# Moving 46 of 96 up-projection units of an MLP into the attention loop before it, with the intermediate kept in DRAM scratch

## The chip, the cores and the metric

One core of a Trainium2 chip runs the whole program. The metric is device time in microseconds (us), the median of several executions. The kernel before takes about 370 us. In runs on a single core an execution counts as slow when it is over 1.5% above the fastest of its kernel.

Engine names in the profile: PE is the matmul engine (PEld its weight loads), DVE the vector engine, ACT the engine for exp and tanh, SP the engine that issues most DMAs.

## The reference, cut to what matters

```python
# attention: B=4, H=8 heads, S=768, D=64; block-sparse mask (blocks of 32)
scores = where(mask, q @ k.T / sqrt(D), -1e9)
attn   = softmax(scores);  out = attn @ v
x = out.transpose(0, 2, 1, 3).reshape(3072, 512)
# MLP
h = x @ w_in                        # 3072 x 2048
g = h * (1 / (1 + exp(-beta * h)))
return g @ w_out                    # 3072 x 512
```

The kernels write the third line as h * (1 + tanh(beta * h / 2)) and take the factor 0.5 into `w_out`; so their MLP needs a tanh and a multiply.

## The kernel before

It first runs a loop over the 32 (batch, head) pairs, here called heads, and then the MLP, here called the tail. All operands of matmuls are fp16. The parts that matter:

```python
# PSUM of the attention loop: 4 banks scores, 2 tp, 1 av, 1 xtp = all 8
scores_pool (bufs=2), tp_pool (bufs=2), av_pool (bufs=1), xtp_pool (bufs=1)

for idx in range(n_bh + 1):
    # ... load q, k, v; cast; 6 + 6 PE transposes of q and k into tp tiles, copy to qa, ka ...
    for kc in range(6):
        sc = scores_pool.tile([128, 768], FP32)
        # two matmuls, 512 and 256 columns
        nc.scalar.activation(out=et[:, kc, :], in_=sc, func=AF.Exp, scale=SCALE)
    # of the previous head: 36 AV matmuls, reciprocal, scale into xstage;
    # every second head: 6 PE transposes of xstage
    xtp = xtp_pool.tile([128, 6, 128], FP16, tag="xtp")
    # ... transposes into xtp, copied to xT_sb (x transposed, all in SBUF)

attn_psum_ctx.close()
for tg in range(6):                     # 512 tokens each
    for ffc in range(16):               # one "unit": 4 matmuls of 512 columns
        # hp (PSUM) = w_in chunk x xT
        nc.scalar.activation(out=t_sb, in_=hp, func=AF.Tanh, scale=beta_h_sb[:, ffc])
        nc.vector.scalar_tensor_tensor(out=g_sb[:, ffc, :], in0=t_sb, scalar=1.0,
                                       in1=hp, op0=ALU.add, op1=ALU.mult)
    for tsub in range(4):               # 16 matmuls g x w_out, copy, store
        ...
```

The kernel's framework puts the instructions of each engine into an order of its own, by a static plan, and it is not that of the program text. A tile's buffers are handed out in rotation within its pool and tag.

The softmax here doesn't subtract the row's maximum and nothing guards it: scores larger than these inputs give would overflow.

## Time and profile before

| stretch of the profiled run (368.8 us) | length | what sets its pace |
|---|---|---|
| loading, mask, first transposes | 25 us | DMA, dependencies |
| attention loop, to the last scaled output at 198.3 us | 173 us | ACT: 5.12 us per head (heads 10 to 31) |
| tail | 170 us | PE: 12 blocks of 64 matmuls, 13.8 us each |

"Us per head" here and below is the mean distance between the instructions that scale the attention output, from the 10th to the 31st of them. "Attention ends" is the start of the 32nd.

The page of the kernel before, its second part: the busy share of each engine in 40 slices of the span, in tenths.

```profile
PE   0338999898999999999998999999999999999995
ACT  0035889777899888889985812812812812812810
DMA  7995364788444453645300002002002002002002
```

Up to slice 21 ACT is the engine that is nearly full; after it PE is, and ACT works only in bursts. The PE row shows nine tenths in attention too, but matmuls overlap in it: a matmul of 512 columns is recorded as 382 ns long, while the next one starts after 216 ns. The Trainium skill, "Perfetto Trace Analysis", section "Identifying the Most-Contended Engine", warns that matmul busy time says little about how near PE is to its limit; the table of stretches agrees here, because PE is "busy" 71 of 74 us while ACT sets the pace:

```profile
110.00:184.00 74.00, 71.24 (x921) 48.55 (x918) 37.26 (x104) 66.03 (x89) 0.00 (x0) 1.00 0.49 111
198.50:365.20 166.70, 166.62 (x773) 75.35 (x771) 82.87 (x122) 65.95 (x96) 0.00 (x0) 1.00 0.10 37
```

The columns are: stretch, length, then busy us and number of instructions of PE, PEld, DVE, ACT and POOL, the granted PE clock, the DMA share and GB/s. In the second row PE has no hole: the tail is PE work from end to end. The chain of waits, in order of time, says the same at its end:

```profile
323.68 13.81 PE op L195 x64
337.49 13.81 PE hp L181 x64
351.30 13.83 PE op L195 x64
```

64 matmuls in 13.81 us are 216 ns each, so a unit is 0.86 us.

### The profile page before, as it was taken

What the parts mean: (1) busy time and instruction counts of PE and PEld (TensorE: products, weight loads), DVE (VectorE), ACT (ScalarE), POOL (GpSimd) and SP (SyncE); (2) the same over time, 40 slices, a digit from 0 to 9 for tenths busy, and PEclk for the clock granted to TensorE, in tenths of its full rate; (3) what the DMA queues carried; (4) which work ended last, traced back from release to release, by engine and by line L of the source; (5) the groups of instructions that cost most, each with busy time, mean ns of one, the idle gap of its engine ahead of it and who ended that gap; (6) DMA issues with size and microseconds to landing.
All of it is one profiled execution on the core that took longest, in us unless ns stands there. A gap on an engine that the chain in (4) does not pass through costs nothing.

```text
span 368.8 us, 6884 instructions
## 1 busy us (share of the span) xinstructions
PE 333.2 (90%) x2785; PEld 186.8 (51%) x2785; DVE 184.8 (50%) x392; ACT 212.2 (58%) x289; POOL 4.9 (1%) x16
## 2 busy tenths in 40 slices
PE   0338999898999999999998999999999999999995
PEld 0214666556566666666665444444444444444442
DVE  2475445665544454655443833833733733733731
ACT  0035889777899888889985812812812812812810
POOL 5000000000000000000000000000000000000000
PEclk9999999999999999999998999999999999999999
DMA  7995364788444453645300002002002002002002
GB/s 234 261 314 125 79 171 109 204 204 197 110 109 92 107 130 87 152 90 126 87 2 2 0 28 88 1 28 87 0 28 88 0 28 87 0 28 87 1 28 87
DMA packets 83652, 34.01 MB, mean 92 GB/s; under 512 B 77988, under 2 KB 77988, under 8 KB 83108
## 3 DMA queue, kind: packets, MB, share of 16 engines
q1 hardware_dynamic: 78804, 25.17, 27.1%
q10 hardware_dynamic: 4816, 8.40, 6.8%
q8 instruction: 22, 0.36, 0.5%
q14 instruction: 10, 0.08, 0.1%
HBM read 27.27 MB, written 6.29 MB: 91 GB/s over the span
## 4 chain that ended last, share of the span: by engine, by line
PE 65%; ACT 17%; DMA 9%; DVE 4%; issue 3%; SPq 0%; ACTq 0%; DVEq 0%
PE hp L181 23%; PE op L195 22%; ACT et_140 L256 9%; ACT et_141 L256 9%; PE sc L250 8%; PE av L265 5%; PE tp L238 4%; PE sc L253 3%; DMA st_317<-in_q_dram 3%; DMA st_180<-in_k_dram 2%; DMA st_813<-in_q_dram 1%; DMA st_1411<-in_k_dram 1%; DMA st_1117<-in_k_dram 1%; PE xtp L284 1%; DVE qaug_119 L240 1%
## 5 line engine op out<-in xcount | busy, mean ns | idle before, releaser
L186 ACT ACTIVATE t_sb<-hp,beta_h_sb 128x512 f16<-128x512 f32 x96 | 66.0, 687 | 89.8 <-PE hp L181 89.8
L181 PE MATMUL hp<-xT_sb,w_in_sb 128*128 128x512 f16 x384 | 85.0, 382 | 0.0
L195 PE MATMUL op<-w_out_sb,g_sb 128*128 128x512 f16 x384 | 83.9, 379 | 0.0
L256 ACT ACTIVATE et_140<-sc 128x768 f16<-128x768 f32 x96 | 73.2, 809 | 16.4 <-PE sc L253 15.3
L256 ACT ACTIVATE et_141<-sc 128x768 f16<-128x768 f32 x96 | 72.5, 809 | 11.5 <-PE sc L253 10.8
L188 DVE SCALAR_TENSOR_TENSOR g_sb<-t_sb,hp 128x512 f16<-128x512 f16 x96 | 66.0, 688 | 20.3 <-ACT t_sb L186 20.3
L181 PEld LDWEIGHTS <-w_in_sb 128*128 128x128 f16 x384 | 37.7, 99 | 45.3 <-issue 0.8
L195 PEld LDWEIGHTS <-g_sb 128*128 128x128 f16 x384 | 37.5, 98 | 45.3
L200 DVE COPY osb<-op 128x512 f32<-128x512 f32 x24 | 16.6, 692 | 62.0 <-PE op L195 62.0
L273 DVE RECIPROCAL recip<-av 128x6 f32<-128x6 f32 x32 | 6.3, 196 | 67.8 <-PE av L265 67.8
L265 PEld LDWEIGHTS <-et_141 128*128 128x128 f16 x576 | 27.4, 99 | 12.5 <-DVE xstage L274 1.6
L265 PEld LDWEIGHTS <-et_140 128*128 128x128 f16 x576 | 28.0, 100 | 10.9 <-issue 2.5
L250 PE MATMUL sc<-qaug_119,kaug_120 88*128 88x512 f16 x66 | 26.5, 403 | 1.9 <-ACT et_141 L256 1.1
L250 PE MATMUL sc<-qaug_126,kaug_127 88*128 88x512 f16 x66 | 26.1, 398 | 2.1 <-ACT et_141 L256 1.0
L250 PE MATMUL sc<-qaug_133,kaug_134 88*128 88x512 f16 x60 | 22.8, 382 | 1.3 <-ACT et_141 L256 0.7
L253 PE MATMUL sc<-qaug_119,kaug_120 88*128 88x256 f16 x66 | 18.8, 285 | 0.0
L253 PE MATMUL sc<-qaug_126,kaug_127 88*128 88x256 f16 x66 | 18.6, 283 | 0.0
L274 DVE TENSOR_TENSOR xstage<-av,recip 128x384 f16<-128x384 f32 x32 | 17.6, 551 | 0.1
L253 PE MATMUL sc<-qaug_133,kaug_134 88*128 88x256 f16 x60 | 16.3, 271 | 0.0
L256 ACT ACT_TABLE_LOAD x1 | 1.3, 1283 | 22.1 <-DVE maskT_110 L109 22.1
L265 PE MATMUL av<-vaug_121,et_140 128*128 128x65 f16 x216 | 12.9, 203 | 0.3 <-ACT et_140 L256 0.3
L265 PE MATMUL av<-vaug_128,et_141 128*128 128x65 f16 x216 | 11.7, 200 | 0.8 <-ACT et_141 L256 0.5
(283 smaller groups left out, 263.9 us busy)
## 6 DMA issues: line engine op xcount, KB each, us to landing
out_dram<-osb SPq DMA_DIRECT2D x24, 256.0 KB, 2.0
w_in_st<-in_moe_w_in_dram ACTq DMA_DIRECT2D x4, 1024.0 KB, 6.7
w_out_st<-in_moe_w_out_dram ACTq DMA_DIRECT2D x8, 512.0 KB, 3.7
st_168<-in_q_dram SPq DMA_DIRECT2D x1, 192.0 KB, 8.8
st_180<-in_k_dram SPq DMA_DIRECT2D x1, 192.0 KB, 8.9
vst_192<-in_v_dram SPq DMA_DIRECT2D x1, 192.0 KB, 9.0
st_222<-in_q_dram SPq DMA_DIRECT2D x1, 192.0 KB, 2.6
st_234<-in_k_dram SPq DMA_DIRECT2D x1, 192.0 KB, 3.0
```

Of the source, the lines that this page charges most:

```text
L181: nc.tensor.matmul(hp, lhsT=w_in_sb[:, c, ffc * P:(ffc + 1) * P], rhs=xT_sb[:, c, tg * 512:(tg + 1) * 512], start=(c == 0), stop=(c == N_D ...
L186: nc.scalar.activation(out=t_sb, in_=hp, func=AF.Tanh, bias=0.0, scale=beta_h_sb[:, ffc:ffc + 1])
L188: nc.vector.scalar_tensor_tensor(out=g_sb[:, ffc, :], in0=t_sb, scalar=1.0, in1=hp, op0=ALU.add, op1=ALU.mult)
L195: nc.tensor.matmul(op, lhsT=g_sb[:, ffc, tsub * P:(tsub + 1) * P], rhs=w_out_sb[:, ffc, :], start=(ffc == 0), stop=(ffc == N_FFC - 1))
L200: nc.vector.tensor_copy(out=osb, in_=op)
L238: nc.tensor.transpose(out=tp[:, c, :], in_=st16[:, c, :], identity=identity[:, 0:P])
L250: nc.tensor.matmul(sc[:, 0:512], lhsT=ka[0:CROWS, kc * P:(kc + 1) * P], rhs=qa[0:CROWS, 0:512], start=True, stop=True)
L253: nc.tensor.matmul(sc[:, 512:S], lhsT=ka[0:CROWS, kc * P:(kc + 1) * P], rhs=qa[0:CROWS, 512:S], start=True, stop=True)
L256: nc.scalar.activation(out=et[:, kc, :], in_=sc, func=AF.Exp, bias=0.0, scale=SCALE)
L265: nc.tensor.matmul(av[:, qc, :], lhsT=pet[:, kc, qc * P:(qc + 1) * P], rhs=pva[:, kc, :], start=(kc == 0), stop=(kc == NKC - 1))
L273: nc.vector.reciprocal(out=recip, in_=av[:, :, D])
L274: nc.vector.tensor_tensor(out=xstage[:, :, (ph % 2) * D:(ph % 2 + 1) * D], in0=av[:, :, 0:D], in1=recip[:, :].to_broadcast([P, NQC, D]), o ...
```

## The change

The intent is to use PE's free time in the ACT-bound attention loop: 46 of the 96 units (two per head in heads 9 to 31) run there. Their h is copied to SBUF as fp16, stored to a scratch in DRAM, and loaded again for tanh and the multiply. The units left in the tail take the same way through DRAM. To find a PSUM bank for the moved units, the change gives up the bank of `xtp`, whose tiles now come from the two buffers of the q and k transposes.

```diff
+    h_dram = dram_pool.tile([N_TG * N_FFC, P, 512], FP16, name="h_dram")
-    xtp_pool = attn_psum_ctx.enter_context(
-        tc.tile_pool(name="xtp_psum", bufs=1, space=bass.MemoryType.PSUM))
+    xtp_pool = tp_pool
+    hf_pool = attn_psum_ctx.enter_context(
+        tc.tile_pool(name="hf_psum", bufs=1, space=bass.MemoryType.PSUM))
+    def emit_h_front(tg, ffc, h_pool):
+        hp = h_pool.tile([P, 512], FP32, tag="hfp", name="hfp")
+        # ... the 4 matmuls ...
+        hst = moe_sbuf.tile([P, 512], FP16, tag="hst", name="hst")      # 3 buffers
+        nc.vector.tensor_copy(out=hst, in_=hp)
+        nc.sync.dma_start(out=h_dram[tg * N_FFC + ffc], in_=hst)
+    def emit_h_back(tg, ffc, g_sb):
+        hld = moe_sbuf.tile([P, 512], FP16, tag="hld", name="hld")      # 3 buffers
+        nc.sync.dma_start(out=hld, in_=h_dram[tg * N_FFC + ffc])
+        # ... tanh and multiply as before, from hld instead of PSUM ...
+    hf_sched = {}
+    for it in range(9, 17):
+        hf_sched[it] = [(0, 2 * (it - 9)), (0, 2 * (it - 9) + 1)]
+    # ... heads 17 to 24: group 1; heads 25 to 31: 14 units of group 2
     # in the loop: one unit after the scores of a head, one after the AV part
-            xtp = xtp_pool.tile([P, NQC, P], FP16, tag="xtp", name="xtp")
+            xtp = xtp_pool.tile([P, NQC, P], FP16, tag="tp", name="xtp")
     # tail: the units left of one later group, then tanh/multiply and w_out of group tg
```

More of the change, by code (lines that the diff above doesn't have):

```diff
@@ L165 @@
         tc.tile_pool(name="av_psum", bufs=1, space=bass.MemoryType.PSUM))
-    xtp_pool = attn_psum_ctx.enter_context(
-        tc.tile_pool(name="xtp_psum", bufs=1, space=bass.MemoryType.PSUM))
-    hin_pool = None
+    xtp_pool = tp_pool
+    hf_pool = attn_psum_ctx.enter_context(
+        tc.tile_pool(name="hf_psum", bufs=1, space=bass.MemoryType.PSUM))
     moe_sbuf = ctx.enter_context(tc.tile_pool(name="moe_sbuf", bufs=3))
@@ L174 @@
     xstage = None
-    def emit_moe_group(tg, h_pool, o_pool):
-        g_sb = moe_sbuf.tile([P, N_FFC, 512], FP16, tag="g_sb", name="g_sb")
-        for ffc in range(N_FFC):
-            hp = h_pool.tile([P, 512], FP32, tag="hp", name="hp")
-            for c in range(N_DMC):
-                nc.tensor.matmul(hp,
-                                 lhsT=w_in_sb[:, c, ffc * P:(ffc + 1) * P],
-                                 rhs=xT_sb[:, c, tg * 512:(tg + 1) * 512],
-                                 start=(c == 0), stop=(c == N_DMC - 1))
-            t_sb = moe_sbuf.tile([P, 512], FP16, tag="t_sb", name="t_sb")
-            nc.scalar.activation(out=t_sb, in_=hp, func=AF.Tanh,
-                                 bias=0.0, scale=beta_h_sb[:, ffc:ffc + 1])
-            nc.vector.scalar_tensor_tensor(out=g_sb[:, ffc, :], in0=t_sb,
-                                           scalar=1.0, in1=hp,
-                                           op0=ALU.add, op1=ALU.mult)
-        for tsub in range(4):
-            op = o_pool.tile([P, D_MODEL], FP32, tag="op", name="op")
-            for ffc in range(N_FFC):
-                nc.tensor.matmul(op,
-                                 lhsT=g_sb[:, ffc, tsub * P:(tsub + 1) * P],
-                                 rhs=w_out_sb[:, ffc, :],
-                                 start=(ffc == 0), stop=(ffc == N_FFC - 1))
-            osb = moe_sbuf.tile([P, D_MODEL], FP32, tag="osb", name="osb")
-            nc.vector.tensor_copy(out=osb, in_=op)
-            row0 = tg * 512 + tsub * P
-            nc.sync.dma_start(out=out[row0:row0 + P, :], in_=osb)
@@ new lines, in emit_h_front @@
+    def emit_h_front(tg, ffc, h_pool):
+        hp = h_pool.tile([P, 512], FP32, tag="hfp", name="hfp")
+        for c in range(N_DMC):
+            nc.tensor.matmul(hp,
+                             lhsT=w_in_sb[:, c, ffc * P:(ffc + 1) * P],
+                             rhs=xT_sb[:, c, tg * 512:(tg + 1) * 512],
+                             start=(c == 0), stop=(c == N_DMC - 1))
+        hst = moe_sbuf.tile([P, 512], FP16, tag="hst", name="hst")
+        nc.vector.tensor_copy(out=hst, in_=hp)
+        nc.sync.dma_start(out=h_dram[tg * N_FFC + ffc], in_=hst)
@@ new lines, in emit_h_back @@
+    def emit_h_back(tg, ffc, g_sb):
+        hld = moe_sbuf.tile([P, 512], FP16, tag="hld", name="hld")
+        nc.sync.dma_start(out=hld, in_=h_dram[tg * N_FFC + ffc])
+        t_sb = moe_sbuf.tile([P, 512], FP16, tag="t_sb", name="t_sb")
+        nc.scalar.activation(out=t_sb, in_=hld, func=AF.Tanh,
+                             bias=0.0, scale=beta_h_sb[:, ffc:ffc + 1])
+        nc.vector.scalar_tensor_tensor(out=g_sb[:, ffc, :], in0=t_sb,
+                                       scalar=1.0, in1=hld,
+                                       op0=ALU.add, op1=ALU.mult)
@@ new lines, in emit_o_unit @@
+    def emit_o_unit(tg, tsub, o_pool, g_sb):
+        op = o_pool.tile([P, D_MODEL], FP32, tag="op", name="op")
+        for ffc in range(N_FFC):
+            nc.tensor.matmul(op,
+                             lhsT=g_sb[:, ffc, tsub * P:(tsub + 1) * P],
+                             rhs=w_out_sb[:, ffc, :],
+                             start=(ffc == 0), stop=(ffc == N_FFC - 1))
+        osb = moe_sbuf.tile([P, D_MODEL], FP32, tag="osb", name="osb")
+        nc.vector.tensor_copy(out=osb, in_=op)
+        row0 = tg * 512 + tsub * P
+        nc.sync.dma_start(out=out[row0:row0 + P, :], in_=osb)
@@ L204 @@
+    hf_sched = {}
+    for it in range(9, 17):
+        hf_sched[it] = [(0, 2 * (it - 9)), (0, 2 * (it - 9) + 1)]
+    for it in range(17, 25):
+        hf_sched[it] = [(1, 2 * (it - 17)), (1, 2 * (it - 17) + 1)]
+    for it in range(25, 32):
+        hf_sched[it] = [(2, 2 * (it - 25)), (2, 2 * (it - 25) + 1)]
     pending_wcast = None
@@ L257 @@
                                  bias=0.0, scale=SCALE)
+        hf_units = hf_sched.get(idx, [])
+        if hf_units:
+            emit_h_front(hf_units[0][0], hf_units[0][1], hf_pool)
       if prev_state is not None:
@@ L291 @@
       if idx < n_bh:
+        for (tg_, ffc_) in hf_units[1:]:
+            emit_h_front(tg_, ffc_, hf_pool)
         prev_state = (b, h, et, va)
@@ L295, with emit_group_back, emit_group_out @@
     with (
-        tc.tile_pool(name="h_psum", bufs=4, space=bass.MemoryType.PSUM) as h_tail_pool,
-        tc.tile_pool(name="o_psum", bufs=4, space=bass.MemoryType.PSUM) as o_tail_pool,
-    ):
-        for tg in range(N_TG):
-            emit_moe_group(tg, h_tail_pool, o_tail_pool)
+        tc.tile_pool(name="hl_psum", bufs=3, space=bass.MemoryType.PSUM) as hl_pool,
+        tc.tile_pool(name="o_psum", bufs=4, space=bass.MemoryType.PSUM) as o_pool,
+    ):
+        fronted = set()
+        for us in hf_sched.values():
+            fronted.update(us)
+        left_by_group = {tg: [f for f in range(N_FFC) if (tg, f) not in fronted]
+                         for tg in range(N_TG)}
+        groups_with_left = [tg for tg in range(N_TG) if left_by_group[tg]]
+        g_tiles = {}
+        def emit_group_back(tg):
+            g_sb = moe_sbuf.tile([P, N_FFC, 512], FP16, tag="g_sb", name="g_sb")
+            g_tiles[tg] = g_sb
+            for ffc in range(N_FFC):
+                emit_h_back(tg, ffc, g_sb)
+        def emit_group_out(tg):
+            for tsub in range(4):
+                emit_o_unit(tg, tsub, o_pool, g_tiles[tg])
+        li = 0
+        for tg in range(N_TG):
+            if li < len(groups_with_left):
+                lg = groups_with_left[li]
+                for f in left_by_group[lg]:
+                    emit_h_front(lg, f, hl_pool)
+                li += 1
+            emit_group_back(tg)
+            emit_group_out(tg)
 _INS = ['q', 'k', 'v', 'sampled_blocks', 'moe_w_in', 'moe_w_out', 'moe_beta']
```

## The prediction

> **What bounds the kernel now** (span 368.8 us; timeline, table of stretches).
> - 0 to 25 us: loading and mask set-up.
> - 25 to 198 us: attention, bound by ACT. From 110 to 184 us ACT is busy 66.0 of 74 us; 89 exps give one per 0.83 us, 5.0 us per head. PE's nine tenths are pipelined time. From start-to-start times I estimate what PE issues per head: 12 score matmuls 1.92 us, 36 AV matmuls at 32 ns 1.15 us, 15 transposes at 57 ns 0.86 us; sum 3.9 us. About 1.1 us per head is free.
> - 198 to 365 us: the MoE tail, bound by PE. The chain of waits is PE alone: 12 blocks of 64 matmuls in 13.81 us (216 ns each), no holes.
>
> **What the change does.** It moves 46 of 96 up-projection units (4 matmuls, 0.86 us) into heads 9 to 31: 39.7 us of PE work leaves the tail. Every unit, also the 50 left in the tail, now pays a PSUM-to-SBUF copy on DVE (0.69 us, like the output copies), a 128 KB store and a 128 KB load before tanh and multiply: 25 MB of extra DMA, 66 us of extra DVE.
>
> **Attention, costed.** Two units add 1.73 us of PE to a head: 3.9 + 1.73 + 0.3 of switching gaps ("issue" waits at the transposes) = 5.9 us, above ACT's 5.0, so these heads turn PE-bound: 0.9 us longer each, 21 us over 23 heads. I also expect tanh work of the first groups to be pulled into attention (the program already issues loads far ahead of their place, and three g buffers exist); some 40 tanh there load ACT to about 5.9 us too, and two full engines stall each other. I take 27 us of growth (18 to 40): attention ends near 225 us.
>
> **Tail, costed.** PE: 384 down-projection matmuls 83 us + 50 units 43 us = 126 us. DVE, if nothing is pulled forward: 50 copies 35 us, 96 multiplies at 0.6 us (estimate) 58 us, 24 output copies 17 us: 109 us. The spill has three load buffers: load, tanh, multiply, buffer free. The Trainium skill, "DMA: Bandwidth & Descriptors", section "Anatomy of one DMA", gives a fixed cost of about 2.0 us; this trace agrees: the 256 KB output stores land in 2.0 us median. Estimate: 2.1 + 0.65 + 0.6 + 0.4 of hand-overs = 3.7 us over three buffers = 1.25 us per unit, 120 us for 96 units, close to the PE limit; units pulled into attention relieve it. I take 131 us for the tail, 4 us for the end.
>
> Sum: 225 + 131 + 4 = 360 us of span, 361 us timed; the risk leans late, so **363 us**, 349 to 386 in 8 of 10. Faster by over 2% (under 362.5): 0.45; within 2%: 0.35; slower: 0.20.
>
> **What would show it.** Heads 9 to 31 about 6.1 us apart instead of 5.0; exps waiting for score matmuls; last head near 225 us. Tail: PE still the chain, about 130 us; if instead PE waits for the multiply, that for tanh and that for the h load, the three-buffer loop is the bound. DMA busy in the tail, near 0.1 before, rises to 0.4 or more. Multiply and tanh no slower than 690 ns.
>
> **What would make it wrong.** Slower: stores and loads of the scratch ordered coarsely against each other, so that groups serialize (then far over 390); tanh queued ahead of exps but waiting for late loads; the SP queue holding loads behind stores that wait for copies. Faster: attention grows 15 us or less and the tail sits at its 126 us floor: about 348 us.

## The result, and the profile after

The change measured 362.68 us median (359.86 to 363.95, 20 runs) against 369.97 us for the kernel before (40 runs). The ratio of the fast runs is 0.9799, 95% interval 0.9779 to 0.9819; it is faster than the kernel before, but since the interval holds 0.98, the verdict at the 2% threshold is "unclear". Ratios here are the mean time of one kernel's fast runs over that of the other's in the same rounds, so not quite the ratio of the quoted medians.

| profiled run | before | after | difference |
|---|---|---|---|
| us per head, heads 10 to 31 | 5.12 | 6.47 | +1.35 |
| attention ends | 198.3 | 230.5 | +32.2 |
| from there to the end | 170.5 | 131.6 | -38.9 |
| span | 368.8 | 362.1 | -6.7 |

The 46 units are 39.7 us of PE work. They left the tail entirely (-38.9), and 32.2 of it came back as a longer attention. The page after, the same rows:

```profile
PE   0339988989999999999999999999999999999995
ACT  0027786578889789788888988511432442452000
DMA  7994558547567666666676742225654763763212
```

The ACT row of attention looks much as before, but part of its work is now tanh: of the 64.5 us that ACT is busy from 110 to 184 us, exps are 49.8 (69 of them, against 89 before). The DMA row now has work in the tail. The table of stretches after (columns as before):

```profile
110.00:184.00 74.00, 72.98 (x808) 45.59 (x806) 59.12 (x131) 64.51 (x93) 0.00 (x0) 1.00 0.67 175
232.80:359.00 126.20, 124.71 (x574) 55.93 (x572) 78.33 (x124) 35.73 (x51) 0.00 (x0) 1.00 0.47 153
```

The tail is still PE work almost without holes, now 126 us. Only 51 of the 96 tanh run there (the count in the ACT column); the other 45 have been pulled forward into attention. The costliest groups show the price of the detour (line, engine, operation, tiles, shapes, count, then busy us and mean ns of one, then the idle time before them and its releaser):

```profile
L194 ACT ACTIVATE t_sb<-hld,beta_h_sb 128x512 f16<-128x512 f16 x96 | 66.7, 720 | 67.4 <-DMA hld<-h_dram 37.1
L196 DVE SCALAR_TENSOR_TENSOR g_sb<-t_sb,hld 128x512 f16<-128x512 f16 x96 | 64.0, 684 | 13.3 <-ACT t_sb L194 12.9
L187 DVE CAST hst<-hfp 128x512 f16<-128x512 f32 x96 | 64.0, 686 | 9.4 <-PE hfp L182 5.1
```

The copy is 64 us of new DVE work. Reading h as fp16 from SBUF made the multiply hardly shorter (684 ns, 688 before) and tanh longer (720 ns, 687 before). The DMA issues (KB each, median us to landing):

```profile
h_dram<-hst SPq DMA_DIRECT2D x96, 128.0 KB, 1.9
hld<-h_dram SPq DMA_DIRECT2D x96, 128.0 KB, 2.3
```

### The profile page after: what moved, and what is told of

Read it like the earlier page. It is cut to its first block, busy times and chain, and to the rows that moved or that the text cites. A ratio compares the mean times of both kernels' runs of the same rounds, so it can differ in the third digit from the quotient of the medians.

```text
span 362.1 us, 7349 instructions
## 1 busy us (share of the span) xinstructions
PE 326.7 (90%) x2785; PEld 184.3 (51%) x2785; DVE 237.6 (66%) x488; ACT 206.3 (57%) x289; POOL 4.9 (1%) x16
## 3 DMA queue, kind: packets, MB, share of 16 engines
q1 hardware_dynamic: 106452, 50.35, 49.8%
## 4 chain that ended last, share of the span: by engine, by line
PE 66%; DMA 12%; ACT 10%; DVE 7%; issue 3%; SPq 0%; DVEq 0%; ACTq 0%
PE op L203 19%; PE hfp L182 15%; PE sc L266 12%; PE av L285 8%; PE tp L254 7%; ACT et_142 L272 6%; PE sc L269 5%; DMA h_dram<-hst 3%; DMA hld<-h_dram 3%; ACT et_141 L272 3%; DMA st_318<-in_q_dram 3%; DVE hst L187 3%; DMA st_181<-in_k_dram 2%; PE xtp L304 2%; DVE g_sb L196 2%
## 5 line engine op out<-in xcount | busy, mean ns | idle before, releaser
L194 ACT ACTIVATE t_sb<-hld,beta_h_sb 128x512 f16<-128x512 f16 x96 | 66.7, 720 | 67.4 <-DMA hld<-h_dram 37.1
L182 PE MATMUL hfp<-xT_sb,w_in_sb 128*128 128x512 f16 x384 | 101.2, 379 | 0.9 <-DVE hst L187 0.6
L272 ACT ACTIVATE et_142<-sc 128x768 f16<-128x768 f32 x96 | 70.7, 811 | 23.4 <-PE sc L269 20.7
L272 ACT ACTIVATE et_141<-sc 128x768 f16<-128x768 f32 x96 | 70.3, 815 | 11.6 <-PE sc L269 11.6
L196 DVE SCALAR_TENSOR_TENSOR g_sb<-t_sb,hld 128x512 f16<-128x512 f16 x96 | 64.0, 684 | 13.3 <-ACT t_sb L194 12.9
L187 DVE CAST hst<-hfp 128x512 f16<-128x512 f32 x96 | 64.0, 686 | 9.4 <-PE hfp L182 5.1
L182 PEld LDWEIGHTS <-w_in_sb 128*128 128x128 f16 x384 | 35.6, 97 | 37.0 <-issue 2.6
L285 PE MATMUL av<-vaug_122,et_141 128*128 128x65 f16 x216 | 12.8, 202 | 0.0
```

The lines of the kernel that those rows point to most:

```text
L182: nc.tensor.matmul(hp, lhsT=w_in_sb[:, c, ffc * P:(ffc + 1) * P], rhs=xT_sb[:, c, tg * 512:(tg + 1) * 512], start=(c == 0), stop=(c == N_D ...
L187: nc.vector.tensor_copy(out=hst, in_=hp)
L194: nc.scalar.activation(out=t_sb, in_=hld, func=AF.Tanh, bias=0.0, scale=beta_h_sb[:, ffc:ffc + 1])
L285: nc.tensor.matmul(av[:, qc, :], lhsT=pet[:, kc, qc * P:(qc + 1) * P], rhs=pva[:, kc, :], start=(kc == 0), stop=(kc == NKC - 1))
```

## The experiments

Twelve kernels ran, in three calls; kernels of one call shared their chip and their runs of the kernel before (medians 368.63, 369.57 and 370.30 us). All gave correct results. In e1 and e2 one of four executions was slow and is left out of the ratio, in e6 three of four. All stage numbers below come from the profiled run of each.

Theory A was: PE decides everywhere; what is gained is the moved PE time that falls into free PE slots of attention. Rivals: B, the round trip through DRAM eats the gain; C, the tanh pulled into attention stalls the exps.

| run | what it is | median us | ratio (95%) | us per head | attention ends | rest |
|---|---|---|---|---|---|---|
| (before) | | 369.97 | 1 | 5.12 | 198.3 | 170.5 |
| (the change) | 46 moved | 362.68 | 0.9799 | 6.47 | 230.5 | 131.6 |
| e1_move0 | change, 0 moved | 394.93 | 1.0688 (1.0637, 1.0738) | 5.65 | 212.2 | 180.2 |
| e2_move23 | change, 23 moved | 374.82 | 1.0092 (1.0024, 1.0159) | 5.82 | 217.8 | 156.4 |
| e3_no_spill | 46 moved, tanh from PSUM | 373.94 | 1.0132 (1.0090, 1.0175) | 6.93 | 242.8 | 129.8 |
| e4_hold_tanh | change, no tanh in attention | 380.72 | 1.0312 (1.0261, 1.0363) | 6.54 | 233.2 | 147.0 |
| e5_shared_tp | before, xtp in tp's buffers | 385.71 | 1.0448 (1.0401, 1.0495) | 5.65 | 214.1 | 169.6 |
| e6_xtp_in_hf | change, xtp in moved units' bank | 368.46 | none | 6.82 | 236.9 | 129.8 |
| e6b_xtp_in_av | change, xtp in AV's bank | 359.32 | 0.9726 (0.9689, 0.9762) | 6.35 | 228.3 | 129.2 |
| e7_hold_8buf | e4 with 8 load buffers | 368.75 | 0.9967 (0.9919, 1.0014) | 6.54 | 231.0 | 133.9 |
| e12_sbuf_0 | repaired, no DRAM, 0 moved | 367.56 | 0.9938 (0.9892, 0.9984) | 5.15 | 195.9 | 169.5 |
| e10_sbuf_23 | repaired, no DRAM, 23 moved | 366.29 | 0.9884 (0.9838, 0.9931) | 5.84 | 214.6 | 150.6 |
| e8_sbuf_46 | repaired, no DRAM, 46 moved | 361.35 | 0.9767 (0.9719, 0.9815) | 6.31 | 225.2 | 133.8 |
| e11_spill_23_8buf | e2 with both repairs | 368.10 | 0.9943 (0.9888, 0.9999) | 5.74 | 211.9 | 155.5 |

"Rest" is the profiled span minus the attention end.

### First call: dose, scratch, tanh

**e1_move0.** Nothing is moved; everything else of the change stays.

```diff
-    hf_sched = {}
-    for it in range(9, 17): ...      # and the two loops after it
+    hf_sched = {}
```

> All 96 units stay in the tail, but each still goes through the copy, the store and the load. Theory A (PE alone decides; what the change gains is the moved PE time that fell into slots where PE was free): attention ends near 198 us as before, the tail is 166 us of PE, total 366 to 376 us, like the kernel before. Theory B (the round trip through DRAM itself costs time and eats the gain): over 380 us.

It took 394.93 us, over 380 as rival B expected. But two things went wrong at once. The rest took 180.2 us, 10 more than in the kernel before: its waits are for the scratch loads.

```profile
ACT t_sb L194 <- DMA hld<-h_dram: 78.5, 64, 7.4
DVE g_sb L196 <- ACT t_sb L194: 32.7, 39, 2.4
PEld L203 <- DVE g_sb L196: 20.5, 45, 1.8
```

This view lists who waited for whom: us in total, times, longest. Here PE waits for the multiply, the multiply for tanh, and tanh for the load, in the tail (213 to 390 us).

The other thing was a surprise: attention also grew, from 198 to 212 us, although no unit ran in it. The timeline shows why. PE, over one boundary between two heads:

```profile
134.80 0.51 PE L298 MATMUL xtp<-identity,xstage 128*128 128x128 f16 x6 [0.38 <-DVE xstage L288]
135.24 0.52 PE L248 MATMUL tp<-identity,st 128*64 128x128 f16 x6
135.69 0.46 PE L279 MATMUL av<-vaug,et 128*128 128x65 f16 x9
136.08 0.52 PE L248 MATMUL tp<-identity,st 128*64 128x128 f16 x6
136.54 0.94 PE L279 MATMUL av<-vaug,et 128*128 128x65 f16 x24
137.32 0.38 PE L260 MATMUL sc<-qaug,kaug 88*128 88x512 f16 x1
```

and ACT at the same time:

```profile
133.07 2.25 ACT L266 ACTIVATE et<-sc 128x768 f16<-128x768 f32 x3
137.91 8.86 ACT L266 ACTIVATE et<-sc 128x768 f16<-128x768 f32 x12 [2.58 <-PE sc L263]
```

The transposes of the attention output (xtp) stand ahead of the transposes of the next head's q and k (tp), and they wait for the finished output of the head before. So the next head's scores start late and ACT idles 2.58 us, every second head. That xtp now takes its tile from the two tp buffers was my suspect: theory P. The times fit it: DVE empties xtp's tile from 135.35 to 135.91 us, and the second batch of tp, which needs a free one of the two buffers, starts at 136.08.

**e2_move23.** One unit per head in heads 9 to 31.

```diff
+    for it in range(9, 25):  hf_sched[it] = [(0, it - 9)]
+    for it in range(25, 32): hf_sched[it] = [(1, it - 25)]
```

> One unit per head instead of two, 23 units moved. Theory A: per head PE then needs 3.9 + 0.86 + about 0.6 of gaps = 5.4 us against 5.0 before, so attention grows by at most 10 us (ends near 206) while the tail sheds 20 us: total 354 to 360 us, at least as good as 46 units. If every unit gains the same small amount, 366 us, halfway between the kernels.

It missed: 374.82 us, worse than the change and 0.9% over the kernel before. Counted from e1_move0, the first 23 units lengthened attention by 5.6 us and the second 23 by another 12.7, so the dose does act through attention as theory A says; but the base from which it acts was not the kernel before.

**e3_no_spill.** tanh and the multiply read PSUM directly; no copy, no scratch; the group buffers (three of them) take the result in attention.

```diff
-        nc.vector.tensor_copy(out=hst, in_=hp)
-        nc.sync.dma_start(out=h_dram[tg * N_FFC + ffc], in_=hst)
+        nc.scalar.activation(out=t_sb, in_=hp, func=AF.Tanh, ...)
+        nc.vector.scalar_tensor_tensor(out=g_sb[:, ffc, :], in0=t_sb, ..., in1=hp, ...)
```

> 46 units moved, but tanh and multiply read the matmul's PSUM directly into the group buffer as in the kernel before; no scratch, no copy, no extra DMA. Theory A: PE is full in attention either way, 358 to 366 us, attention ends near 230. Theory B (copies, DMA and round trip cost): 340 to 352 us. A third possibility: with one PSUM bank for these units and tanh queued behind exps, PE waits for the bank and it is slower, 368 us or more.

The third expectation held: 373.94 us, 6.93 us per head. Without any copy or DMA attention is slower, not faster, but something else changed too: until tanh and the multiply are done, the one PSUM bank of the moved units is not free. The multiply waits for tanh in heads 10 to 31:

```profile
DVE g_sb L193 <- ACT t_sb L191: 39.2, 31, 2.7
```

I did not separate that from the longer ACT queue, so this run alone does not decide about B in attention. e8 below, without scratch and without tanh there, does: 6.31 us per head, against 6.35 with the scratch in e6b.

**e4_hold_tanh.** The change, but tanh takes its scale from a copy that depends on the last attention output.

```diff
+    nc.vector.scalar_tensor_tensor(out=beta_late, in0=xT_sb[:, N_DMC - 1, N_TOK - N_FFC:N_TOK],
+                                   scalar=0.0, in1=beta_h_sb, op0=ALU.mult, op1=ALU.add)
-  scale=beta_h_sb[:, ffc:ffc + 1]
+  scale=beta_late[:, ffc:ffc + 1]
```

> The change as it is, but tanh is made to depend on the last attention output (its scale is read from a copy made after it), so no tanh runs in the attention loop. Theory A: PE alone sets the heads' pace, 6.4 to 6.5 us per head stays, attention ends 229 to 233 us; the tail needs 96 trips of the three-buffer loop at 1.25 us = 120 us beside 126 us of PE: total 362 to 372 us. Rival C (tanh on ACT stalls the exps, two full engines): heads fall to 5.9 to 6.0 us, attention ends near 219 us, total 350 to 360 us.

C falls: with no tanh in attention the pace stays at 6.54 us per head (6.47 with it), and ACT merely idles, waiting for scores over these heads:

```profile
ACT et L272 <- PE sc L269: 46.2, 21, 3.1
```

The total of 380.72 us, however, missed theory A's 362 to 372: the rest took 147.0 us. Its waits (234 to 380 us):

```profile
ACT t_sb L194 <- DMA hld<-h_dram: 62.6, 64, 4.9
PEld L203 <- DVE g_sb L196: 32.5, 63, 2.4
```

### Second call: the shared buffers and the load loop

**e5_shared_tp.** The kernel before with one edit.

```diff
-    xtp_pool = attn_psum_ctx.enter_context(tc.tile_pool(name="xtp_psum", bufs=1, ...))
+    xtp_pool = tp_pool
-            xtp = xtp_pool.tile([P, NQC, P], FP16, tag="xtp", name="xtp")
+            xtp = xtp_pool.tile([P, NQC, P], FP16, tag="tp", name="xtp")
```

> The kernel before with one edit: the transposes of the attention output take their PSUM tile from the two buffers of the q and k transposes, as in the change; nothing else moves. Theory P (the shared buffers hold back the next head's transposes, ACT starves 2.6 us every second head, as the run with nothing moved shows): attention ends at 210 to 214 us instead of 198, total 380 to 386 us. Rival (the slower attention of that run came from the other instruction order or the stores): no change, 368 to 372 us.

Theory P holds: 385.71 us, attention ends at 214.1 us, and nothing but this edit differs from the kernel before. The waits of ACT for scores in heads 10 to 31, first in the kernel before (two lines for its two et buffers), then here:

```profile
ACT et_140 L256 <- PE sc L253: 5.9, 6, 1.3
ACT et_141 L256 <- PE sc L253: 5.1, 8, 1.2
```

```profile
ACT et L254 <- PE sc L251: 28.2, 11, 2.6
```

11 holes of up to 2.6 us, one per pair of heads, against 11.0 us in 14 small waits. The Trainium skill, "Perfetto Trace Analysis", section "Optimization Strategy", says that consistent bubbles on the engine that should be full can mean that there isn't enough SBUF or PSUM for the next tile; this trace agrees.

**e6_xtp_in_hf** and **e6b_xtp_in_av.** The change, with xtp in the bank of the moved units, or in the bank of the AV product, so that q and k have two buffers to themselves again.

```diff
-            xtp = xtp_pool.tile([P, NQC, P], FP16, tag="tp", name="xtp")
+            xtp = hf_pool.tile([P, NQC, P], FP16, tag="hfp", name="xtp")     # e6
+            xtp = av_pool.tile([P, NQC, P], FP16, tag="av", name="xtp")      # e6b
```

> The change, but the transposes of the attention output share the bank of the moved units, and q and k have their two buffers to themselves again. Theory P: heads 9 to 31 fall from 6.47 to about 6.0 us (5.7 of PE issue plus gaps), attention ends at 219 to 224 us, total 350 to 356 us. If PE is simply full there, so that the shared buffers no longer matter once two units per head are in, nothing changes: 360 to 364 us, attention ends near 231.

> As the previous one, but sharing the bank of the AV product. Theory P: the same gain, 350 to 356 us, less 1 or 2 us if the moved units had waited for their bank there. If PE is simply full: 360 to 364 us.

e6 is inconclusive: three executions took 368.4 to 368.9 us and were slow, one took 361.77, and its profile is of the slow kind. e6b took 359.32 us, 6.35 us per head. So the repair is worth 3 us, not the 8 to 12 that theory P expected. The 16 us that sharing costs alone are not a cost on top of the moved units. Sharing costs 0.53 us per head with nothing moved (e5 against the kernel before), but 0.08 with one unit per head (e2 against e11 below) and 0.12 with two (the change against e6b). I read this as the moved matmuls filling the holes that sharing makes.

**e7_hold_8buf.** e4 with a pool of 8 buffers for `hld`.

```diff
+    hld_pool = ctx.enter_context(tc.tile_pool(name="hld_pool", bufs=8))
-        hld = moe_sbuf.tile([P, 512], FP16, tag="hld", name="hld")
+        hld = hld_pool.tile([P, 512], FP16, tag="hld", name="hld")
```

> The run with tanh held back until attention is over, with 8 load buffers in place of 3. If the three-buffer loop bounds its tail (147 us for 96 units, 1.53 us each, against 126 us of PE): the tail shrinks to 126 to 132 us, total 359 to 366 us. If it is DVE or the order of its work: no change, 378 to 383 us.

The rest fell from 147.0 to 133.9 us, and the wait of tanh for loads left the top of the list (231 to 365 us):

```profile
ACT t_sb L196 <- DVE g_sb L198: 33.0, 26, 2.5
DVE osb L210 <- PE op L205: 23.3, 9, 2.8
PEld L205 <- DVE g_sb L198: 6.5, 18, 0.7
```

So the three-buffer loop was the bound in e4. There the 96 tanh start 1.44 us apart on average (235.3 to 371.7 us); the 1.53 us in the expectation above also counts the time before the first and after the last. In e7 they start 1.02 us apart. The median of 368.75 us is a little above the expected range, the tail's 133.9 us too; PE still waits here and there for the multiply.

### Third call: the dose in a repaired structure

These kernels share the AV bank for xtp. In the three "sbuf" kernels a moved unit's h is copied straight into its slot of the group buffer in SBUF and waits there for tanh, which then works in place; units of the tail go from PSUM to tanh as in the kernel before. There is no scratch.

```diff
-        nc.vector.tensor_copy(out=hst, in_=hp)
-        nc.sync.dma_start(out=h_dram[tg * N_FFC + ffc], in_=hst)
+        if moved: nc.vector.tensor_copy(out=g_tiles[tg][:, ffc, :], in_=hp)
+        else:     act(tg, ffc, hp)             # tanh and multiply from PSUM
+   # in the tail, for the moved units of group tg:
+        act(tg, ffc, g_tiles[tg][:, ffc, :])
```

> Repaired structure, nothing moved: no scratch in DRAM, all 96 units straight from PSUM in the tail as in the kernel before, the output transposes share the bank of the AV product. A base for the two runs beside it. Expected like the kernel before, 366 to 373 us, attention ends at 196 to 202 us. If sharing that bank costs as sharing the transposes' buffers did, 375 us or more.

> Repaired structure, one unit per head moved; its h is copied into the group buffer in SBUF and waits there for tanh; no DRAM. Theory A (gain is moved PE time in free PE slots): heads 5.0 to 5.5 us, attention ends near 206 us, tail 146 us, total 352 to 359 us. If the first 23 units gain nothing either (as the run with 23 in the changed kernel seemed to say): 366 us or more.

> Repaired structure, two units per head moved, h in SBUF, no DRAM. Against the run with the AV bank shared and the DRAM scratch (359.3 us) this takes away the 25 MB of DMA and half of the copies only. If the scratch costs nothing once tanh runs ahead: 356 to 361 us. If it still cost: 350 us or less.

> The run with 23 units through DRAM (374.8 us), with both repairs: the AV bank shared and 8 load buffers. If those two explain why half the units did worse than none: 352 to 361 us. If the round trip has another cost: over 366 us.

With nothing moved (e12) the structure equals the kernel before: 5.15 us per head, attention ends at 195.9, so sharing AV's bank is harmless. With 46 units (e8) it reaches 361.35 us, inside the range that says the scratch costs nothing once tanh runs ahead; its interval overlaps that of e6b with the scratch. But the two differ in more than the scratch: in e6b 44 tanh run in attention, in e8 none, and e8's shorter attention (225.2 against 228.3 us) is offset by a longer rest (133.8 against 129.2), so what the scratch costs is not isolated. e8 does exclude two rivals for the pace of the heads: from 110 to 184 us ACT is busy only 51.5 us and DVE 44.7, against 64.5 and 59.1 in the change, and yet a head takes 6.31 us.

```profile
110.00:184.00 74.00, 72.16 (x820) 46.18 (x817) 44.72 (x109) 51.50 (x71) 0.00 (x0) 1.00 0.42 95
```

But 23 units (e10) gave only 366.29 us, and the repaired version with scratch (e11) 368.10, in the range that I had read as another cost of the round trip. Its rest is indeed 155.5 us against 150.6 in e10, and tanh waits there for copies and loads; its attention is 2.7 us shorter, and the intervals of the two overlap. Theory A's dose prediction, that the first 23 units gain most, fell a second time, now without the shared buffers and without the load loop as excuses. The first unit per head lengthens a head by 0.69 us of its 0.86; the second by 0.47.

The timeline of e10 shows where the first unit goes. PE, from the last scores of one head to the first of the next:

```profile
146.81 0.39 PE L265 MATMUL sc<-qaug,kaug 88*128 88x512 f16 x1
147.03 0.27 PE L268 MATMUL sc<-qaug,kaug 88*128 88x256 f16 x1
147.24 0.69 PE L253 MATMUL tp<-identity,st 128*64 128x128 f16 x9
147.86 0.39 PE L182 MATMUL hfp<-xT_sb,w_in_sb 128*128 128x512 f16 x1
148.08 0.50 PE L303 MATMUL xtp<-identity,xstage 128*128 128x128 f16 x6
148.42 0.81 PE L182 MATMUL hfp<-xT_sb,w_in_sb 128*128 128x512 f16 x3
149.07 0.38 PE L265 MATMUL sc<-qaug,kaug 88*128 88x512 f16 x1
```

and ACT:

```profile
143.67 4.54 ACT L271 ACTIVATE et<-sc 128x768 f16<-128x768 f32 x6 [0.88 <-PE sc L268]
149.65 2.96 ACT L271 ACTIVATE et<-sc 128x768 f16<-128x768 f32 x4 [1.44 <-PE sc L268]
```

Between two score pairs PE works 2.0 us on transposes and the unit. Two score buffers give ACT at most two exps to live on, about 1.5 us, and part of that is gone before. So ACT idles at nearly every head boundary. Its waits in heads 10 to 31, in e10 and then in e12:

```profile
ACT et L271 <- PE sc L268: 25.9, 20, 1.8
```

```profile
ACT et L267 <- PE sc L264: 10.3, 12, 1.3
```

The free PE time of a head is not one slot of 1.1 us but many small ones between score pairs, and the unit was put where the loop has none. In e8 one of a head's two units is spread, one or two matmuls at a time, between score pairs (at 144.05, 144.81 and 145.40 us, for instance), and there the step to two units cost less than the step to one. That placement is the cause is read from the traces. In e2 much of the one unit is spread like this, and it added only 0.17 us per head to e1_move0; but that base has the holes of the shared buffers, which a unit can fill wherever it stands. No run tried a spread unit in the repaired structure, so this stays argued and not shown.

Part of the price needs no placement, and I had overlooked it: PE has less free time than 1.1 us. In the traces of all 14 kernels every change between the q and k transposes (tp, which load 128x64 weights) and any other matmul, in either direction, delays the next start by 90 ns or more, with a median of 95 ns. The lines above show it: six xtp transposes before hfp take 0.34 us (148.08 to 148.42), six before tp in e1_move0 take 0.44 (134.80 to 135.24). The kernel before makes 5.0 such changes per head, 0.53 us; that leaves about 0.6 us free of the 1.1, less than one unit.

**What beats both kernels.** e6b_xtp_in_av, at a ratio of 0.9726 against 0.9799 for the change, each to the kernel before in its own rounds; the two did not run side by side, but the intervals do not overlap.

## Why the prediction was right or wrong

The time was right: 363 predicted, 362.68 measured. Point by point:

- **The tail is PE's and stays so: right.** 126 us of PE predicted, a stretch of 126.2 us with hardly a hole measured; 131.6 us with the end, against 131 + 4 predicted.
- **The moved work fits only partly and turns these heads PE-bound: right in kind, mis-sized.** Predicted 6.1 us per head and an end near 225 us; measured 6.47 and 230.5, so growth was 32 us, not 27. Two terms were off. Issue times of 3.9 + 1.73 us in a head of 6.47 leave 0.8 us, where I had put 0.3 us of switching gaps: by the start times, 0.30 us are the changes to and from the q and k transposes, as predicted, and most of the rest, 0.48 us, lies before score matmuls; what these wait for I did not separate. And I costed 1.1 us of free PE time as one slot and left the 0.53 us of such changes in the kernel before out of it, while e10 and e12 show that one unit of 0.86 us alone already costs 0.69.
- **Overlooked: the shared transposes' buffers.** The prediction does not mention that edit. Alone it costs 16 us (e5). It did little harm in the change (e6b: 3 us), as I read it because the moved matmuls fill the holes it makes.
- **"Some 40 tanh" pulled into attention: right, 45.** It matters more than I said: with none pulled forward the same kernel takes 380.72 us (e4).
- **"Two full engines stall each other": wrong.** With no tanh in attention the pace did not improve (e4: 6.54 against 6.47 us).
- **The three-buffer loop: right mechanism, size too small.** I estimated 1.25 us per unit; e4 shows 1.44 where it binds, and 8 buffers remove it (e7). In the change itself it does not bind, because of the 45 tanh that ran ahead. The multiply was estimated at 0.6 us and measured 684 ns.
- **"Multiply and tanh no slower than 690 ns": wrong for tanh.** The multiply took 684, tanh 720 on average. DMA in the tail rose to 0.47, as predicted. Of the fears, a coarse order of the scratch (far over 390 us) did not come; tanh waited for loads in attention for 2.3 us only; the SP queue did stand 36.3 us waiting for copies before stores, but PE stayed busy for 124.7 of 126.2 us in the tail.

So the total was right partly by luck: attention ended 5.5 us later than predicted, the rest took 3 us less, and 2 us had been added to the costed 361 us only because "the risk leans late".

## What to carry to other kernels

Moving work into another engine's shadow gains only what falls into real free slots of the moved work's own engine: count the time lost at changes between kinds of matmul before calling it free, and ask how long each slot is and whether the next critical instruction waits behind the moved block (the last point is argued here, not shown). When a change borrows a buffer to make room, test the borrowing alone on the old kernel; here it cost 16 us by itself, more than twice what the whole change won, and the moved work hid most of it. A round trip through a scratch does little harm while its consumer runs ahead of it or has buffers enough (e4 against the change and e7): count loop latency over buffers against the pace it must keep.

## What the Trainium skill lacked or had wrong

- "VectorE: DVE Perf Modes", section "The perf-mode tier table", has no row for scalar_tensor_tensor. Here 128x512 took 684 ns with both tensors fp16 in SBUF and 688 ns with one of them fp32 in PSUM, so moving its source out of PSUM won nothing.
- "DMA: Bandwidth & Descriptors", section "Anatomy of one DMA", gives a fit of about 2.0 us plus the bytes over 436 GB/s for DMAs issued from GpSimd. Taken over to DMAs issued by SP, it would be an estimate of 2.3 us for 128 KB and 2.6 us for 256 KB. The traces show 2.3 us for the 128 KB loads, but 1.9 us for the 128 KB stores and 2.0 us for the 256 KB output stores (medians), so here it fits the loads and not the stores.
- No page that I read gives a time for changing between kinds of matmul on PE. Here every change to or from the q and k transposes (128x64 weights) delayed the next start by 90 ns or more, 95 ns in the median of 1748 changes in 14 traces. Changes among the other kinds have no such least cost: score to AV, hfp to score and xtp to hfp follow at the plain spacing in the median.
